# Attention scores of a head pair in one run of half-array products, and a planner with new operation lengths

## The chip, the cores and the metric

The kernel runs on one core of one Trainium2 chip. The metric is the device time of one execution in microseconds; the median of three runs is given. Before the change it is 209.5 us.

## What is computed

The reference has two stages. The first is a recurrent linear attention over 4 batches, 8 heads, 768 positions and a head size of 64. Each head has a decay gamma, and

```
state = gamma * state + k[t] v[t]^T
x[t]  = scale * q[t] state
```

The 8 heads side by side make an x of 768 x 512 for each batch. The second stage is a mixer: with `xt` the transpose of x,

```
h   = relu(xt @ w_tok1) @ w_tok2        # 768 -> 256 -> 768, over positions
u   = x + h^T
out = u + relu(u @ w_ch1) @ w_ch2       # 512 -> 1536 -> 512, over channels
```

## The kernel before, in words

**Tiling of the attention.** The recurrence is done in 6 chunks of 128 positions (NC = 6, HC = 3 is half of them). Two heads make a pair, so each batch has 4 pairs, and one call of `front(b, p)` makes all the instructions of one pair p of one batch b. The keys are scaled by powers of the decay (L419 on ScalarE, L421 on VectorE) and cast; the queries are cast (L427, L429) in batches 2 and 3. Both are then transposed so that the head size lies on the partitions, with one head of the pair on partitions 0 to 63 and the other on 64 to 127: by TensorE in batches 0 and 1 (L454, L456, copied out of PSUM at L463), by DMA transposes from the SyncE queue in batches 2 and 3 (L442). The states of the chunks are products of keys and values (L478), run into each other on VectorE (L487, L490: `U`), and scaled into a block-diagonal tile (L501, L503: `r`).

**The scores.** At L521 keys times queries are formed for each chunk: a product that contracts over 64 partitions only, so that it uses half of the array's rows, and the two heads of a pair use the two halves. The products of three chunks of one head fill 384 of the 512 columns of one PSUM bank. The kernel before makes them in two operations for each pair, one for each half of the sequence (`hf`): six products in turns of the two heads, into two banks. VectorE then multiplies each bank by the causal mask and writes it in half precision (L529, `am`). The Y products (L543 with the states, L546 with the masked scores) follow; X is scaled out of PSUM (L559 on ScalarE, L563 on VectorE) and cast (L576).

**The mixer.** The products over positions stay in `front`: L590 (w_tok1), L600 (relu), L648 (w_tok2), an addition at L655, a cast at L663 and a transpose (L682, L688, or by DMA at L672). In batch 0 they take another form (L615, L618, L625, L770). `back(b)` makes the channel part: `widen` (L738 products, L752 relu on ScalarE), and `narrow` (L778 products, L786 additions); batches 2 and 3 use `narrow_seven` (L854, L863, L896), with seven products in place of eight.

**What sets the order.** Nothing runs in the order in which it is written. Each piece of work is an `Op` with its ways (an engine, a time for which the engine is taken, a time until the result is there), what it depends on, and the tiles and banks that it opens. `arrange()` goes through them like a machine: at each step it takes the operation that can start first, of those the one of the best priority, picks the engine that would be done first where there are two ways, and gives each PSUM tile the bank that comes free first. `replay()` runs the finished order again with a model of the DMA queues and so corrects the landing times that `arrange()` uses. After 16 turns the order with the least planned end is emitted. So a time in a tuple like `dict(ACT=(540, 610), DVE=(410, 465))` decides only the order and the engine. `free` holds the time at which each engine is first available.

**Banks.** In batch 0 the front has banks 0 to 6 ("first"); in the later batches it has banks 0 to 4 ("front") and the back has 5 to 7. An operation that opens a bank waits until all that used it before are done.

**Loads.** Keys, queries, values and weights come through the GpSimd queue (L375, L357), each with a cast to half precision, in one fixed order: batch 0, the weights, then batches 1 to 3. Each request waits for the one eight places ahead of it. The same GpSimd also does the casts of L576 and L663. In the first 30 us zero products (L964) fill gaps that the plan leaves on TensorE.

Of the kernel before, what the change touches and what calls it, by code (L numbers as in the profile page):

```python
# [10 lines left out]
FP = mybir.dt.float32  # L11
F16 = mybir.dt.float16
# [5 lines left out]
def kernel(  # L18
# [11 lines left out]
    nc = tc.nc  # L30
# [23 lines left out]
    SEM = 80  # L54
    XB, XU = 2, 3
    EARLY, BOTH_FIRST, SEVEN = 0, 1, 2
    ops = []
# [25 lines left out]
    def replay(order):  # L83
# [17 lines left out]
        at = {e: 0 for e in lines}  # L101
        free = dict(PE=0, ACT=2500, DVE=0, POOL=850, SP=700)
        dmas = {e: [] for e in ("SP", "POOL", "ACT")}
# [73 lines left out]
    def arrange():  # L177
        free = dict(PE=0, ACT=2500, DVE=0, POOL=850, SP=700)
        gens = [0, 0, 0]
# [87 lines left out]

    def act(n, scaled=False):
        t = 186 + (93 if scaled else 0) + 5 * n // 6
        return t - 60, t + 20  # L270

    def dve(n, per=1.04):
        return int(140 + n * per), int(170 + n * per)

# [92 lines left out]
    rcount = [0]  # L367

    def load(b, p):
        got = []  # L370
        for tag, src in (("kf", k), ("qf", q), ("v16", v)):
            s = Slot(tag)

            def emit(s=s, src=src):
                nc.gpsimd.dma_start(out=tile_of(s, [P, 2, NC, D], F16),  # L375
                                    in_=src[b, 2 * p:2 * p + 2].rearrange("h (c p) d -> p (h c) d", p=P))
            pr = (0, -2) if (b, p) == (0, 0) and tag == "kf" else (0, b, p)
            got.append((s, request(pr, 1040, emit, (96, 13.2), [s])))
        loads[b, p] = got

    def front(b, p):
# [32 lines left out]
        def emit(e, js):  # L414
            t = opened(K, [P, NC, 2, D], F16)
            for j in js:
# [3 lines left out]
                else:  # L420
                    nc.vector.tensor_scalar(t[:, :, j], KF.tile[:, j], gk[:, h:h + 1], None, ALU.mult)  # L421
        kl = parts(emit, dict(ACT=(540, 610), DVE=(410, 465)), [kd, g_op], K, KF, ([0], [1]))

# [6 lines left out]
        if b < XB:  # L430
            ql = [qd]
        else:
            ql = parts(emit, dict(ACT=(780, 860), DVE=(500, 550)), [qd], Q, QF, (slice(0, 2),))

# [3 lines left out]
        def turn(src, dst, dep):  # L438
            if b >= XB:
                def emit():  # L440
                    t = tile_of(dst, [P, S], F16)
                    nc.sync.dma_start_transpose(out=t.rearrange("d (c t) -> d c t", t=P),  # L442
                                                in_=flat(src.tile))
                o = Op((0, b, p, 0), [("SP", 100, 100, emit)], dep, [dst], [src], dma=(48, 24))
                return [o, o]
            T = Slot(FA)

            def emit():
                tp = tile_of(T, [P, 1024], F16)
                for c in range(NC):  # L450
                    o = tp[:, c * P:(c + 1) * P]
                    if src is QF:
                        for j in range(2):
                            nc.tensor.transpose(o[j * D:(j + 1) * D], src.tile[:, j, c], ident16)  # L454
                    else:
                        nc.tensor.transpose(o, src.tile[:, c].rearrange("p h d -> p (h d)"), ident16)  # L456
            t = op(one("PE", (600, 760) if src is QF else (340, 500), emit), dep + [ident_op], [T], [src])

            def emit(e, hs):
                d, o = opened(dst, [P, S], F16), T.tile[:, :S]  # L460
                d = d.rearrange("d (f t) -> d f t", f=2)[:, hs]
                o = o.rearrange("d (f t) -> d f t", f=2)[:, hs]
                (nc.scalar.copy if e == "ACT" else nc.vector.tensor_copy)(d, o)  # L463
            if last:
                return parts(emit, dict(ACT=act(S // 2), DVE=dve(S // 2, 0.54)), [t], dst, T,
                             (slice(0, 1), slice(1, 2)))
            return 2 * parts(emit, dict(ACT=act(S), DVE=dve(S, 0.54)), [t], dst, T, (slice(0, 2),))
# [6 lines left out]
        def emit():  # L474
            st = tile_of(ST, [P, 512], FP)
            for c in range(NC - 1):
                for j in range(2):
                    nc.tensor.matmul(st[j * D:(j + 1) * D, c * D:(c + 1) * D], K.tile[:, c, j],  # L478
                                     V.tile[:, j, c], start=True, stop=True)
        pp = op(one("PE", (320, 470), emit), kl + [vl, two_before], [ST], [K, V])  # L480
        prev = None
        for c in range(NC - 1):
            def emit(c=c):
                o = ST.tile[:, c * D:(c + 1) * D]
                if c == 0:
                    U = tile_of(US, [P, NC - 1, D], FP)
                    nc.vector.tensor_copy(U[:, 0], o)  # L487
                else:
                    U = US.tile
                    nc.vector.scalar_tensor_tensor(U[:, c], U[:, c - 1], gp[:, p:p + 1], o,  # L490
                                                   ALU.mult, ALU.add)
            prev = op(one("DVE", (215, 270), emit), [pp, prev], [US] if c == 0 else [],
                      [ST, US] if c else [ST])

        def emit(e, j):
# [6 lines left out]
            else:  # L502
                nc.vector.tensor_scalar(RS.tile[r, :, r], US.tile[r], g128[2 * p + j], None, ALU.mult)  # L503
        r0 = op(either(lambda e, f=emit: f(e, 0), ACT=(400, 470), DVE=(460, 490)),
                [prev, r16_op], [RS], [US])
        r1 = op(either(lambda e, f=emit: f(e, 1), ACT=(400, 470), DVE=(460, 490)),
                [prev, r0], [], [US, RS])

        AM = [Slot("am") for _ in range(4)]
        am_ops = []  # L510
        for hf in range(2):
            A = [Slot(FA), Slot(FA)]

            def emit(hf=hf, A=A):
                a = [tile_of(A[j], [P, 512], FP)[:, :HC * P].rearrange("p (i t) -> p i t", t=P)
                     for j in range(2)]
                for i in range(HC):
                    t = slice((hf * HC + i) * P, (hf * HC + i + 1) * P)
                    for j in range(2):
                        r = slice(j * D, (j + 1) * D)  # L520
                        nc.tensor.matmul(a[j][:, i], KT.tile[r, t], QT.tile[r, t],  # L521
                                         start=True, stop=True)
            a = op(one("PE", (300, 420), emit), [kt[hf], qt[hf], two_before], A, [KT, QT])
            for j in range(2):
                def emit(hf=hf, j=j, A=A):
                    am = tile_of(AM[2 * hf + j], [P, HC, P], F16)
                    src = A[j].tile[:, :HC * P].rearrange("p (i t) -> p i t", t=P)
                    m = mask1.rearrange("p (o t) -> p o t", o=1).to_broadcast([P, HC, P])
                    nc.vector.tensor_tensor(am, src, m, ALU.mult)  # L529
                am_ops.append(op(one("DVE", (500, 560), emit), [a, mask1_op], [AM[2 * hf + j]], [A[j]]))  # L530
        X16 = Slot("x16")
        x_ops, cast_ops = [], []
        for hf in range(2):
            Y = Slot(FA)

            def emit(hf=hf, Y=Y):
                y = tile_of(Y, [P, 512], FP)
                R = RS.tile
                for i in range(HC):
# [5 lines left out]
                    for j in range(2):  # L545
                        nc.tensor.matmul(o[:, j * D:(j + 1) * D], AM[2 * hf + j].tile[:, i],  # L546
                                         V.tile[:, j, c], start=(c == 0), stop=(c == 0 or j == 1))
            y = op(one("PE", (360, 510), emit), am_ops[2 * hf:2 * hf + 2] + [r0, r1, vl], [Y],
                   [QT, RS, V, AM[2 * hf], AM[2 * hf + 1]])
            y_done[b * NP + p] = y  # L550

            def emit(e, hf=hf, Y=Y):
# [8 lines left out]
                else:  # L561
                    gg = gyw[:, 2 * p:2 * p + 2].rearrange("p (o h) d -> p o (h d)", o=1)
                    nc.vector.tensor_tensor(X.tile[:, half(hf), pc], yv, gg.to_broadcast([P, HC, P]),  # L563
                                            ALU.mult)
            ways = either(emit, ACT=(720, 800)) if first else either(emit, ACT=(720, 800), DVE=(520, 580))
            opens = (b, "X") not in first_of
# [6 lines left out]
            def emit(e, hf=hf):  # L573
                if hf == 0:
                    tile_of(X16, [P, NC, P], F16)
                (nc.vector if e == "DVE" else nc.gpsimd).tensor_copy(  # L576
                    X16.tile[:, half(hf)], X.tile[:, half(hf), pc])
            cast_ops.append(op(either(emit, POOL=(460, 530), DVE=(520, 560)),
                               [ev] + cast_ops, [X16] if hf == 0 else [], [X] if hf == 0 else [X, X16]))
# [60 lines left out]
        for hf in range(2):  # L640
# [12 lines left out]
            def emit(hf=hf, T2=T2):  # L653
                xo = X.tile[:, half(hf), pc]
                nc.vector.tensor_tensor(  # L655
                    xo, xo, T2.tile[:, :HC * P].rearrange("p (i d) -> p i d", d=P), ALU.add)
            ad = op(one("DVE", (500, 560), emit), [t2, cast_ops[hf]], [], [T2, X])
            x_done[b, p, hf] = ad

            def emit(e, hf=hf):  # L660
                if hf == 0:
                    tile_of(U16, [P, NC, P], F16)
                (nc.vector if e == "DVE" else nc.gpsimd).tensor_copy(  # L663
                    U16.tile[:, half(hf)], X.tile[:, half(hf), pc])
            casts.append(op(either(emit, POOL=(460, 530), DVE=(520, 560)),
                            [ad] + casts, [U16] if hf == 0 else [], [X] if hf == 0 else [X, U16]))
# [51 lines left out]
    def back(b):  # L718
# [40 lines left out]
        def narrow(sh):  # L759
            H2, rel = h2_of[sh]  # L760
            for i in range(HC):
# [22 lines left out]
                def emit(sh=sh, i=i, A=A, O=O):  # L784
                    o = tile_of(O, [P, C], FP)
                    nc.vector.tensor_tensor(o, X.tile[:, sh * HC + i], A.tile, ALU.add)  # L786
                ad = op(one("DVE", (640, 700), emit), [last] + [x_done[b, p, sh] for p in range(NP)],
                        [O], [A, X])
# [208 lines left out]
```

## Time and profile before

| what | value |
| --- | --- |
| time, median of 3 runs | 209.5 us (208.44 to 209.69) |
| span of the profiled execution | 208.2 us |
| TensorE clock granted | 0.996 |
| first L738, first product of the channel part | 32.2 us |
| L521, score products | 192, 8 runs of twelve and 16 of six |
| L529, maskings | 64, 549 ns each, 33.3 us |
| last L854 | 203.5 us |

A row of the profile's groups gives line, engine and operation, what is written and read, count, busy time and the mean of one; behind the bar stands the idle time of the engine just before. A row of the chain or of the timeline begins with the start in microseconds from the span's start and the length. Matmuls overlap each other, so the distance between two starts says more on TensorE than a record's length.

### The profile page before, as it was taken

To read this page: it belongs to the slowest core of one execution; us is meant where nothing else is said; L and a number is where in the kernel's file an instruction comes from. 1 tells how busy PE (TensorE), PEld (TensorE's weight loads), DVE (VectorE), ACT (ScalarE), POOL (GpSimd) and SP (SyncE) were. 2 spreads that over 40 slices of the span, in tenths; PEclk is the share of its full clock that TensorE was granted. 3 is DMA by queue.
4 is the path that set the end of the run, shared out by engine and by line. 5 is a ranking of instruction groups with operands and counts; after the bars stand their busy time and mean duration, and the time that the engine had idled before them with its cause. 6 is when DMAs were issued, how large, how long until landed. Compare 5 with 4: busy or idle time off the path is not lost.

```text
span 208.2 us, 5030 instructions
## 1 busy us (share of the span) xinstructions
PE 194.7 (94%) x2032; PEld 131.0 (63%) x2032; DVE 126.4 (61%) x331; ACT 115.2 (55%) x250; POOL 79.1 (38%) x111
## 2 busy tenths in 40 slices
PE   7976999999899798999799999999999999999991
PEld 3553785556667365666577566654666887667880
DVE  7597830048798857968487675812007985037972
ACT  3465896578797654476499350730777102776000
POOL 7995963376999643774033124000000000000000
PEclk9999999999999999999999999999999999999998
DMA  7999999999999999999999614302100033000232
GB/s 47 147 158 161 208 206 207 176 156 152 145 149 149 123 186 146 187 125 217 132 183 116 116 50 91 88 0 101 54 0 0 5 139 146 17 3 2 85 120 101
DMA packets 98199, 23.92 MB, mean 115 GB/s; under 512 B 91008, under 2 KB 95104, under 8 KB 98176
## 3 DMA queue, kind: packets, MB, share of 16 engines
q0 software_dynamic: 78720, 13.37, 95.0%
q1 hardware_dynamic: 16000, 3.93, 17.2%
q10 hardware_dynamic: 3456, 6.29, 8.4%
q8 instruction: 16, 0.26, 0.6%
q14 instruction: 7, 0.06, 0.1%
HBM read 26.74 MB, written 6.29 MB: 159 GB/s over the span
## 4 chain that ended last, share of the span: by engine, by line
PE 51%; DMA 34%; POOL 8%; issue 2%; DVE 2%; DVEq 0%; POOLq 0%
PE bank L738 22%; DMA kf<-in_k_dram 14%; PE bank L854 13%; DMA wc<-in_moe_w_ch_dram 8%; PE bank L778 8%; DMA qT<-q 7%; DMA qf<-in_q_dram 4%; POOL kf L375 3%; POOL qf L375 2%; PE bank L590 2%; PE bank L648 2%; POOL v L375 2%; PE bank L521 1%; POOL x L576 1%; PE bank L546 1%
## 5 line engine op out<-in xcount | busy, mean ns | idle before, releaser
L738 PE MATMUL bank<-uT,wc 128*128 128x384 f16 x384 | 67.8, 326 | 0.1
L752 ACT ACTIVATE h<-bank 128x384 f16<-128x384 f32 x96 | 46.6, 488 | 31.0 <-PE bank L738 18.0
L738 PEld LDWEIGHTS <-wc 128*128 128x128 f16 x384 | 36.1, 98 | 24.3 <-issue 0.7
L778 PE MATMUL bank<-wc,h 128*128 128x512 f16 x144 | 37.1, 380 | 0.0
L529 DVE TENSOR_TENSOR am<-bank,mask 128x384 f16<-128x384 f32 x64 | 33.3, 549 | 6.1 <-PE bank L521 6.0
L559 ACT ACTIVATE X<-bank,gy 128x192 f32<-128x192 f32 x48 | 17.2, 416 | 7.7 <-PE bank L546 7.6
L375 POOL DMA_DIRECT2D kf<-in_k_dram x16 | 16.5, 1031 | 9.2 <-DMA qf<-in_q_dram 4.0
L576 POOL CAST x<-X 128x384 f16<-128x384 f32 x28 | 14.1, 518 | 14.0 <-ACT X L559 11.0
L778 PEld LDWEIGHTS <-h 128*128 128x128 f16 x144 | 12.4, 98 | 10.8
L375 POOL DMA_DIRECT2D qf<-in_q_dram x16 | 16.4, 1024 | 5.6 <-DMA wc<-in_moe_w_ch_dram 3.3
L375 POOL DMA_DIRECT2D v<-in_v_dram x16 | 16.3, 1021 | 5.5 <-DMA kf<-in_k_dram 3.5
L419 ACT ACTIVATE k<-kf,gk 128x384 f16<-128x384 f16 x23 | 13.4, 611 | 8.3 <-DMA kf<-in_k_dram 7.2
L490 DVE SCALAR_TENSOR_TENSOR U<-U,gp,bank 128x64 f32<-128x64 f32 x64 | 17.3, 273 | 0.7
L813 DVE TENSOR_TENSOR kf<-h 128x768 f16<-128x768 f16 x6 | 3.3, 558 | 22.4 <-ACT h L752 22.4
L663 POOL CAST u<-X 128x384 f16<-128x384 f32 x22 | 10.8, 509 | 14.2 <-DVE X L655 14.2
L655 DVE TENSOR_TENSOR X<-X,bank 128x384 f32<-128x384 f32 x24 | 12.2, 549 | 6.0 <-PE bank L648 6.0
L854 PEld LDWEIGHTS <-h 128*128 128x128 f16 x144 | 14.1, 98 | 1.9
L590 PE MATMUL bank<-x,wt 128*128 128x128 f16 x192 | 13.8, 219 | 1.4 <-POOL x L576 0.8
L501 ACT ACTIVATE r<-U 64x320 f16<-64x320 f32 x30 | 14.0, 466 | 2.0 <-DVE U L490 1.3
L421 DVE TENSOR_SCALAR k<-kf,gk 128x384 f16<-128x384 f16 x9 | 4.1, 455 | 17.8 <-DMA kf<-in_k_dram 17.7
L786 DVE TENSOR_TENSOR o<-X,bank 128x512 f32<-128x512 f32 x12 | 8.2, 684 | 10.6 <-PE bank L778 10.6
L590 PEld LDWEIGHTS <-wt 128*128 128x128 f16 x192 | 11.8, 98 | 4.1 <-ACT uT L688 1.1
(84 smaller groups left out, 281.9 us busy)
## 6 DMA issues: line engine op xcount, KB each, us to landing
out_dram<-o ACTq DMA_DIRECT2D x24, 256.0 KB, 2.2
kf<-in_k_dram POOLq DMA_DIRECT2D x16, 192.0 KB, 11.4
qf<-in_q_dram POOLq DMA_DIRECT2D x16, 192.0 KB, 12.4
v<-in_v_dram POOLq DMA_DIRECT2D x16, 192.0 KB, 11.9
wc<-in_moe_w_ch_dram POOLq DMA_DIRECT2D x6, 512.0 KB, 15.4
wt<-in_moe_w_tok_dram POOLq DMA_DIRECT2D x2, 384.0 KB, 9.6
kT<-k SPq DMA_TRANSPOSE x8, 8.2
qT<-q SPq DMA_TRANSPOSE x8, 9.7
```

What stands on the lines that cost most here:

```text
L375: nc.gpsimd.dma_start(out=tile_of(s, [P, 2, NC, D], F16), in_=src[b, 2 * p:2 * p + 2].rearrange("h (c p) d -> p (h c) d", p=P))
L419: nc.scalar.activation(t[:, :, j], KF.tile[:, j], AF.Copy, scale=gk[:, h:h + 1])
L490: nc.vector.scalar_tensor_tensor(U[:, c], U[:, c - 1], gp[:, p:p + 1], o, ALU.mult, ALU.add)
L501: nc.scalar.mul(RS.tile[r, :, r], US.tile[r], g128[2 * p + j])
L529: nc.vector.tensor_tensor(am, src, m, ALU.mult)
L559: nc.scalar.mul(X.tile[:, half(hf), h * D:(h + 1) * D], yv[:, :, j * D:(j + 1) * D], gy[:, h:h + 1])
L576: (nc.vector if e == "DVE" else nc.gpsimd).tensor_copy(X16.tile[:, half(hf)], X.tile[:, half(hf), pc])
L590: nc.tensor.matmul(acc[:, jt * P:(jt + 1) * P], wt1[:, i, jt * P:(jt + 1) * P], X16.tile[:, i], start=(i == 0), stop=(i == NC - 1))
L738: nc.tensor.matmul(acc[:, :SH], w[:, ct, (ft % FW) * P:(ft % FW + 1) * P], UT.tile[:, ct, sh * SH:(sh + 1) * SH], start=(ct == 0), stop=(c ...
L752: nc.scalar.activation(H2.tile[:, ft], A.tile[:, :SH], AF.Relu)
L778: nc.tensor.matmul(A.tile, H2.tile[:, ft, i * P:(i + 1) * P], wc2[ft // FW][:, ft % FW], start=(opens and ft == 0), stop=(ft == NF - 1))
L854: nc.tensor.matmul(bank.tile[:, cols], lhs(f, t), rhs(f), start=(f == 0 and not adds), stop=(f == HF - 1), skip_group_check=adds)
```

## The change

The scores of a pair are made in one operation from batch 1 on (`XS = 1`): twelve half-array products in one run, over four banks, where there were two operations of six products over two banks each. `M4 = 3` is the number of chunks in each of the first two banks; with six chunks the other two have three as well. Batch 0 keeps its two operations. The maskings take their bank and their number of blocks from a list, and the Y products look up in `am_of` where a block lies. The aim is that TensorE changes less often between the whole and the half array.

The rest of the change gives the planner other operation lengths, read from a trace, and another first time for the GpSimd queue (1250 for 850) and for the first two loads. The diff, cut:

```diff
+    XS, M4 = 1, 3
...
-        free = dict(PE=0, ACT=2500, DVE=0, POOL=850, SP=700)
+        free = dict(PE=0, ACT=2500, DVE=0, POOL=1250, SP=700)
...
-    def act(n, scaled=False):
-        t = 186 + (93 if scaled else 0) + 5 * n // 6
-        return t - 60, t + 20
+    def act(n):
+        t = 178 + 81 * n // 100
+        return t - 100, t
...
-        return int(140 + n * per), int(170 + n * per)
+        return int(62 + n * per), int(145 + n * per)
...
+    extra = {(0, 0, "kf"): 34, (0, 0, "qf"): 26}
...
-        kl = parts(emit, dict(ACT=(540, 610), DVE=(410, 465)), [kd, g_op], K, KF, ([0], [1]))
+        kl = parts(emit, dict(ACT=(515, 615), DVE=(240, 320)), [kd, g_op], K, KF, ([0], [1]))
...
-            ql = parts(emit, dict(ACT=(780, 860), DVE=(500, 550)), [qd], Q, QF, (slice(0, 2),))
+            ql = parts(emit, dict(ACT=(740, 835), DVE=(340, 390)), [qd], Q, QF, (slice(0, 2),))
...
-            t = op(one("PE", (600, 760) if src is QF else (340, 500), emit), dep + [ident_op], [T], [src])
+            t = op(one("PE", (480, 640) if src is QF else (340, 500), emit), dep + [ident_op], [T], [src])
...
-        pp = op(one("PE", (320, 470), emit), kl + [vl, two_before], [ST], [K, V])
+        pp = op(one("PE", (375, 525), emit), kl + [vl, two_before], [ST], [K, V])
...
-            prev = op(one("DVE", (215, 270), emit), [pp, prev], [US] if c == 0 else [],
+            prev = op(one("DVE", (190, 273), emit), [pp, prev], [US] if c == 0 else [],
...
-        for hf in range(2):
-            A = [Slot(FA), Slot(FA)]
...
-            a = op(one("PE", (300, 420), emit), [kt[hf], qt[hf], two_before], A, [KT, QT])
...
-                am_ops.append(op(one("DVE", (500, 560), emit), [a, mask1_op], [AM[2 * hf + j]], [A[j]]))
+        if b < XS:
+            runs = [[[(j, hf * HC + i) for i in range(HC)] for j in range(2)] for hf in range(2)]
+        else:
+            runs = [[[(j, c) for c in cs] for cs in (range(M4), range(M4, NC)) for j in range(2)]]
+        for blocks in runs:
+            A = [Slot(FA) for _ in blocks]
...
+                for c in sorted({c for _, c in where}):
                     for j in range(2):
...
+                        a, i = where[j, c]
+                        r, t = slice(j * D, (j + 1) * D), slice(c * P, (c + 1) * P)
+                        nc.tensor.matmul(a.tile[:, i * P:(i + 1) * P], KT.tile[r, t], QT.tile[r, t],
                                          start=True, stop=True)
...
+            a = op(one("PE", (370, 500) if len(blocks) == 2 else (545, 680), emit),
+                   [kt[hf] for hf in hfs] + [qt[hf] for hf in hfs] + [two_before], A, [KT, QT])
...
+                mo = op(one("DVE", (66 + 134 * len(bl), 150 + 134 * len(bl)), emit), [a, mask1_op], [M], [A_])
+                for i, jc in enumerate(bl):
+                    am_of[jc] = M, i, mo
...
-            ways = either(emit, ACT=(720, 800)) if first else either(emit, ACT=(720, 800), DVE=(520, 580))
+            ways = either(emit, ACT=(620, 730)) if first else either(emit, ACT=(620, 730), DVE=(475, 557))
```

The lengths of the state scalings (L501), the Y products, the casts (L576, L663) and the additions (L655, L786) are changed in the same manner.

More of the change, by code (lines that the diff above doesn't have):

```diff
@@ L177, in arrange @@
     def arrange():
-        free = dict(PE=0, ACT=2500, DVE=0, POOL=850, SP=700)
+        free = dict(PE=0, ACT=2500, DVE=0, POOL=1250, SP=700)
         gens = [0, 0, 0]
@@ L377, in load @@
             pr = (0, -2) if (b, p) == (0, 0) and tag == "kf" else (0, b, p)
-            got.append((s, request(pr, 1040, emit, (96, 13.2), [s])))
+            got.append((s, request(pr, 1040, emit, (96 + extra.get((b, p, tag), 0), 13.2), [s])))
         loads[b, p] = got
@@ L503, in emit @@
                 nc.vector.tensor_scalar(RS.tile[r, :, r], US.tile[r], g128[2 * p + j], None, ALU.mult)
-        r0 = op(either(lambda e, f=emit: f(e, 0), ACT=(400, 470), DVE=(460, 490)),
+        r0 = op(either(lambda e, f=emit: f(e, 0), ACT=(365, 467), DVE=(400, 480)),
                 [prev, r16_op], [RS], [US])
-        r1 = op(either(lambda e, f=emit: f(e, 1), ACT=(400, 470), DVE=(460, 490)),
+        r1 = op(either(lambda e, f=emit: f(e, 1), ACT=(365, 467), DVE=(400, 480)),
                 [prev, r0], [], [US, RS])
-        AM = [Slot("am") for _ in range(4)]
@@ L510, in front @@
-        am_ops = []
-        for hf in range(2):
-            A = [Slot(FA), Slot(FA)]
[L514 to L518, printed above, removed]
+        AMW = max(HC, M4)
+        AM, am_ops, am_of = [], [], {}
+        if b < XS:
+            runs = [[[(j, hf * HC + i) for i in range(HC)] for j in range(2)] for hf in range(2)]
+        else:
+            runs = [[[(j, c) for c in cs] for cs in (range(M4), range(M4, NC)) for j in range(2)]]
@@ L519, in emit @@
+        for blocks in runs:
+            A = [Slot(FA) for _ in blocks]
+            def emit(blocks=blocks, A=A):
+                where = {jc: (a, i) for a, bl in zip(A, blocks) for i, jc in enumerate(bl)}
+                for a in A:
+                    tile_of(a, [P, 512], FP)
+                for c in sorted({c for _, c in where}):
                     for j in range(2):
-                        r = slice(j * D, (j + 1) * D)
-                        nc.tensor.matmul(a[j][:, i], KT.tile[r, t], QT.tile[r, t],
+                        a, i = where[j, c]
+                        r, t = slice(j * D, (j + 1) * D), slice(c * P, (c + 1) * P)
+                        nc.tensor.matmul(a.tile[:, i * P:(i + 1) * P], KT.tile[r, t], QT.tile[r, t],
@@ L522, in emit @@
                                          start=True, stop=True)
-            a = op(one("PE", (300, 420), emit), [kt[hf], qt[hf], two_before], A, [KT, QT])
[L524 to L529, printed above, removed]
-                am_ops.append(op(one("DVE", (500, 560), emit), [a, mask1_op], [AM[2 * hf + j]], [A[j]]))
+            hfs = [hf for hf in range(2) if any(c // HC == hf for bl in blocks for _, c in bl)]
@@ new lines, in front, with emit @@
+            a = op(one("PE", (370, 500) if len(blocks) == 2 else (545, 680), emit),
+                   [kt[hf] for hf in hfs] + [qt[hf] for hf in hfs] + [two_before], A, [KT, QT])
+            for A_, bl in zip(A, blocks):
+                M = Slot("am")
+                AM.append(M)
+                def emit(bl=bl, A_=A_, M=M):
+                    m = len(bl)
+                    am = tile_of(M, [P, AMW, P], F16)
+                    src = A_.tile[:, :m * P].rearrange("p (i t) -> p i t", t=P)
+                    k_ = mask1.rearrange("p (o t) -> p o t", o=1).to_broadcast([P, m, P])
+                    nc.vector.tensor_tensor(am[:, :m], src, k_, ALU.mult)
+                mo = op(one("DVE", (66 + 134 * len(bl), 150 + 134 * len(bl)), emit), [a, mask1_op], [M], [A_])
+                for i, jc in enumerate(bl):
+                    am_of[jc] = M, i, mo
@@ L545, in emit @@
                     for j in range(2):
[L546 to L549, printed above, removed]
+                        M, m, _ = am_of[j, c]
+                        nc.tensor.matmul(o[:, j * D:(j + 1) * D], M.tile[:, m], V.tile[:, j, c], start=(c == 0), stop=(c == 0 or j == 1))
+            ms = [am_of[j, hf * HC + i] for j in range(2) for i in range(HC)]
+            mine = [M for M in AM if any(M is m[0] for m in ms)]
+            y = op(one("PE", (345 if hf else 290, 500 if hf else 440), emit),
+                   list({id(m[2]): m[2] for m in ms}.values()) + [r0, r1, vl], [Y], [QT, RS, V] + mine)
             y_done[b * NP + p] = y
@@ L577, in emit @@
                     X16.tile[:, half(hf)], X.tile[:, half(hf), pc])
-            cast_ops.append(op(either(emit, POOL=(460, 530), DVE=(520, 560)),
+            cast_ops.append(op(either(emit, POOL=(450, 510), DVE=(462, 548)),
                                [ev] + cast_ops, [X16] if hf == 0 else [], [X] if hf == 0 else [X, X16]))
@@ L656, in emit @@
                     xo, xo, T2.tile[:, :HC * P].rearrange("p (i d) -> p i d", d=P), ALU.add)
-            ad = op(one("DVE", (500, 560), emit), [t2, cast_ops[hf]], [], [T2, X])
+            ad = op(one("DVE", (465, 548), emit), [t2, cast_ops[hf]], [], [T2, X])
             x_done[b, p, hf] = ad
@@ L664, in emit @@
                     U16.tile[:, half(hf)], X.tile[:, half(hf), pc])
-            casts.append(op(either(emit, POOL=(460, 530), DVE=(520, 560)),
+            casts.append(op(either(emit, POOL=(450, 510), DVE=(462, 548)),
                             [ad] + casts, [U16] if hf == 0 else [], [X] if hf == 0 else [X, U16]))
@@ L786, in emit @@
                     nc.vector.tensor_tensor(o, X.tile[:, sh * HC + i], A.tile, ALU.add)
-                ad = op(one("DVE", (640, 700), emit), [last] + [x_done[b, p, sh] for p in range(NP)],
+                ad = op(one("DVE", (605, 687), emit), [last] + [x_done[b, p, sh] for p in range(NP)],
                         [O], [A, X])
```

## The prediction

> **What bounds the kernel now.** I read the page first: busy shares, slices, queues.
>
> ```profile
> PE 194.7 (94%) x2032; PEld 131.0 (63%) x2032; DVE 126.4 (61%) x331; ACT 115.2 (55%) x250; POOL 79.1 (38%) x111
> ...
> PE   7976999999899798999799999999999999999991
> ...
> DMA  7999999999999999999999614302100033000232
> ...
> q0 software_dynamic: 78720, 13.37, 95.0%
> ```
>
> TensorE is nearly always busy, and the DMA rings are full up to slice 22, some 114 us. A busy TensorE is not proof of work, since each record overlaps the next, so I took the distance from one matmul's start to the next as its price. The TensorE timeline gives 0.163 us for L738, 0.216 for L778, 0.056 for the 128-column products of L590, L648 and L682. Counts times these pitches, from the first L738 at 32.2 us to the last L854 at 203.6, come to 164.9 us of work; the stretch lasts 171.4, so 6.5 us in it are waits. Then 4.6 us of additions and the output's store follow. TensorE sets the end, and what can be won is work taken off it, or these waits.
>
> The chain that ended last says what the waits are (start, length, what):
>
> ```profile
> 61.02 18.48 DMA kf<-in_k_dram
> 79.52 0.32 DVE k L421
> 79.84 0.48 DVE X L563
> 80.36 0.32 PE bank L521 x5
> ...
> 91.40 10.62 DMA qT<-q
> 102.02 0.14 issue
> 102.16 0.51 PE bank L521 x12
> ...
> 114.62 4.66 DMA qT<-q
> ```
>
> Two kinds: a load that arrives late and holds VectorE, whose next instruction would have freed a bank for a score run; and a transposed query that reaches the score run itself late. Before 102 us the waits cost 5.8 us: the largest lie at 55 (1.0), 71 to 73 (1.4) and 80.4 (1.2). The one at 102.16 costs 1.3, later ones 0.5. The rows of TensorE's waits agree:
>
> ```profile
> PE bank L521 <- DMA qT<-q: 2.0, 3, 1.2
> ...
> PE bank L521 <- DVE X L563: 1.0, 1, 1.0
> ...
> PE bank L590 <- POOL x L576: 0.8, 1, 0.8
> ```
>
> The score runs themselves, in the timeline (start, us, engine, line):
>
> ```profile
> 83.59 0.59 PE L778 MATMUL bank<-wc,h 128*128 128x512 f16 x2
> 84.12 0.34 PE L521 MATMUL bank<-qT,kT 64*128 64x128 f16 x6
> 84.39 1.04 PE L778 MATMUL bank<-wc,h 128*128 128x512 f16 x4
> ...
> 107.97 0.51 PE L521 MATMUL bank<-qT,kT 64*128 64x128 f16 x12
> 108.41 0.84 PE L590 MATMUL bank<-x,wt 128*128 128x128 f16 x12
> ```
>
> Two L778 take 0.43 us, but the score run starts 0.53 after the first: 0.10 us go into the change from the whole to the half array. Six products then hold TensorE for 0.27 us, twelve for 0.44. So the second six cost 0.17 and about 0.10 is paid on leaving.
>
> **What the skill says.** "TensorEngine Tiling (Array Packing)", Tiling Modes: changing the tiling mode, not merely the tile, drains TensorE. The trace agrees: about 0.10 us at each end of a half-array run. Same page, Restrictions and Gotchas: different row tiles write different PSUM banks and may not use one bank at once. That is why the two heads of a pair have banks of their own, and why one run for the pair takes four. "PSUM — Partial Sum Buffer", Engine vs sequencer instructions: the queues of ScalarE, VectorE and GpSimd are strict FIFO. The chain agrees: at 79.5 us VectorE's L563 stood behind a key scaling that waited for its load. "DMA: Bandwidth & Descriptors", Issuing engines are not separate DMA queues: transfers from all issuers share the same 16 engines and interleave. The trace agrees: a transpose issued at 91.40 landed 10.62 us later, beside the loads.
>
> **The change part by part.**
>
> *The merged run.* With HC = M4 = 3, a bank holds three blocks as before and each of the 64 maskings (L529, 549 ns) keeps its shape: nothing is added or taken on VectorE. Before, eight of the sixteen pairs already have a run of twelve (the four of batch 0, and four later ones which the planner put together); eight have two runs of six. A merge saves 2 x (0.10 + 0.27) - (0.10 + 0.44) = 0.20 us; eight make 1.6. Some half-array runs stand beside others, where entering costs nothing, so I counted in the order of the built programs: half-array groups fall from 48 to 40, entries from the whole array from 39 to 34. That is 8 x 0.10 + 5 x 0.10 = 1.3 us, all of it TensorE work on the path. With the pitches, the work from the first L738 on falls from 164.9 to 163.7 us. I take 1.2.
>
> *The added wait.* A run now opens four of the five front banks at once, and waits for both halves of kT and qT; these come in one transfer or copy in the later batches, so the second costs nothing. On TensorE everything queued behind, the back products too, waits with it; the maskings, then the Y products, wait for the run. In the changed order the TensorE work between a bank's last writer and the score run that reopens it is at least 1.26 us, mostly 1.5 to 5; before, three cases lie at 1.1 to 1.3. The low bound is no wait. The high bound is the shortest succession, pairs 2 and 3 of batch 1, 2.8 us of work apart: four maskings at a pitch of 0.47 take 1.9, and one load in VectorE's queue ahead of them can add 1 us. I take 0, for the reason two parts below.
>
> *The new lengths.* They change no instruction, only the order, and the choice between engines. Query casts on VectorE go from 2 to 6 (0.384 us there, 0.828 on ScalarE), key scalings from 9 to 11 (about 0.32 against 0.61), X scalings from 8 to 5 (0.555). Together with the copies VectorE gets about 1 us more and ScalarE half a us less; both are under 62% busy, so the sums are hidden. Two zero products more (0.16 each) lie in the first 23 us where TensorE waits for loads: nothing.
>
> *The order against the loads.* The rings are full whatever the plan, so I hold the landings and move the work. For a score run, let A be the TensorE work between the first L738 and it. TensorE can't be there before the query lands, so landing minus A is a floor under first L738 plus all waits so far. Batch 3, pair 0: A is 63.9 us before, which gives 102.16 - 63.9 = 38.3, and the end follows: 38.3 + 164.9 + 0.4 of later waits = 203.6, as measured. In the changed order A is 64.7, since the fronts of batches 1 and 2 stand 2 to 4 us later among the back products. The floor is 102.16 - 64.7 = 37.5. All waits before this point, a bank wait included, only eat into a lead which TensorE would have to wait off here; that is why I took 0 above, and why I count nothing for the 2.6 us at 71 to 80 either, though most of them should go. The end is then 37.5 + 163.7 + 0.4 = 201.6: 2.0 us won, 1.2 by less work and 0.8 by the place of the run.
>
> *The query itself.* For that pair the cast ran on ScalarE at 90.54, behind two key scalings and a scaling of X, and its transpose left at 91.40. It is now on VectorE and less than half as long. The transpose can't leave ahead of the pair's kT, which went at 89.75: the gain is between 0 and 1.65 us. I take 1.0. Sum: 3.0 us, 209.5 - 3.0 = 206.5.
>
> **The rivals.**
>
> *A, the waits stay.* The loads come later by what the order gains, because the transposes of the other pairs interleave differently; only the 1.2 us of work go: 208.3. For it: full rings up to 114 us. Against it: the floor's arithmetic, which needs no faster transfer for the 0.8.
>
> *B, slower: the wait moves to VectorE's queue.* Six query casts and eleven key scalings there now wait directly for loads, with maskings and additions behind them. In the changed order the cast of pair 2 of batch 2 stands ahead of the additions of batch 1, the cast of pair 1 ahead of the maskings of batch 1. The case at 79.5 held 2.7 us of idle VectorE and cost TensorE 1.2. If four such come, at 1.3 each, and push back the scalings that feed the transposes so that the floor rises with them, 5.2 us are lost against the 3.0: 211.7. Against it: the plan now expects the first loads 0.4 us later than it did, near to what the trace shows, so it leaves more room.
>
> *C, more won.* If the batch 3 queries of pairs 0 to 2 come early enough, the last one binds: it landed at 119.28, A there is 83.9 in the changed order, floor 119.4 - 83.9 = 35.5, end 35.5 + 163.7 = 199.2, 4.4 us won: 205.1.
>
> **How the numbers follow.** Forecast 206.5 with 0.50; A 208.3 with 0.27; B 211.7 with 0.13; C 205.1 with 0.10. The likeliest is 206.5. The range leaves out most of B and little of C: 204.5 to 210.0. Faster by over 1% means under 207.4: nearly all of the forecast, C and a little of A, less the part of the forecast in which the query gains nothing, 0.55. Same 0.33, slower 0.12.
>
> **What would show it.** In the profile after: score runs of twelve alone, about 0.44 us from start to next start; the maskings still x64 at 549 ns; TensorE's waits between 50 and 81 us well under 4 us; a wait for qT at the first pair of batch 3 (a little before 102 us), and the first L738 about where it was. The prediction is wrong if that wait for qT is absent and another one, on VectorE or a bank, has come instead; if TensorE waits for a bank at score runs; or if qT of batch 3 lands later than 102 us.

## The result, and the profile after

The changed kernel takes 206.4 us (median of 4 runs) against 209.2 us before (a fourth run joined the three): a ratio of 0.987, 95% interval 0.983 to 0.991. Run once more beside the later experiments it gave 0.987 again (0.981 to 0.993). The forecast was 206.5, which was 3.0 us under the 209.5 known then; measured are 2.8. Times and ratios here and below leave out slow executions, those more than 1.5% above the fastest of the same kernel.

The page of the changed kernel: first the busy shares, then the maskings (line, engine, operation, count, busy time, mean ns, idle before), which are L544 now; the score products are L530, the channel products L757, L797 and L873. In the text, L738 and L854 stand for the first and the last kind of channel product in every kernel.

```profile
PE 193.8 (95%) x2034; PEld 132.0 (64%) x2034; DVE 128.2 (63%) x335; ACT 116.0 (57%) x252; POOL 78.4 (38%) x108
...
DMA  6999999999999999999999733202100133000222
...
q0 software_dynamic: 78720, 13.37, 96.6%
...
L544 DVE TENSOR_TENSOR am<-bank,mask 128x384 f16<-128x384 f32 x64 | 32.7, 548 | 3.8 <-PE bank L530 3.7
```

The rings are as full as before, to slice 22; VectorE has 1.8 us more and ScalarE 0.8 more (foreseen were about 1 more and half a us less; both stay hidden), and the maskings have kept their shape. The timeline of TensorE (start, us) shows the merged run among channel products:

```profile
116.64 0.51 PE L530 MATMUL bank<-qT,kT 64*128 64x128 f16 x12
117.08 1.25 PE L797 MATMUL bank<-wc,h 128*128 128x512 f16 x5
```

It is 0.44 us from its start to the next start, the price that a run of twelve had before. All runs have twelve now. What TensorE waited for at the score runs, from the waits (total, times, longest):

```profile
PE bank L530 <- DVE U L493: 0.9, 1, 0.9
...
PE bank L530 <- DMA qT<-q: 0.7, 2, 0.4
```

And the chain that ended last, in the stretch from 60 to 108 us:

```profile
60.75 19.80 DMA kf<-in_k_dram
80.55 0.02 issue
80.57 0.32 DVE k L424
80.89 0.20 DVE U L493
...
81.78 0.47 PE bank L530 x6
...
97.23 9.66 DMA qT<-q
106.90 0.04 issue
106.94 0.51 PE bank L530 x12
```

The first wait is one for a bank: in the middle of a merged run the third bank was still held by state products, whose reader on VectorE stood behind a key scaling that waited for a load. The second is the transposed query of batch 3, pair 1: it landed at 106.90 and the score run began 0.04 us later. Pair 0 had waited for its own query at 100.6 (0.32 us).

From starts and pitches, as in the prediction, TensorE's time from the first L738 (now L757) to the last L854 (now L873) comes apart into work and waits:

| kernel | first L738 | last L854 | work between | waits between |
| --- | --- | --- | --- | --- |
| before | 32.2 | 203.5 | 165.1 | 6.2 |
| changed | 33.3 | 200.1 | 163.8 | 2.9 |
| changed, run again | 33.1 | 201.2 | 163.8 | 4.3 |

Work fell by 1.3 us; the waits fell by 1.9 to 3.3 us; the stretch starts about 1 us later. Each row is one execution: the one of the kernel before took 210.0 us, 0.8 over its median, so its waits may be at the high end.

### The profile page after: what moved, and what is told of

It reads as the page before. It is cut to its first block, busy times and chain, and to the rows that moved or that the text cites. A ratio compares the mean times of both kernels' runs of the same rounds, so it can differ in the third digit from the quotient of the medians.

```text
span 204.8 us, 5035 instructions
## 1 busy us (share of the span) xinstructions
PE 193.8 (95%) x2034; PEld 132.0 (64%) x2034; DVE 128.2 (63%) x335; ACT 116.0 (57%) x252; POOL 78.4 (38%) x108
## 4 chain that ended last, share of the span: by engine, by line
PE 63%; DMA 19%; DVE 10%; POOL 4%; issue 1%; ACT 1%; DVEq 0%; POOLq 0%
PE bank L757 25%; PE bank L873 13%; PE bank L797 11%; DMA kf<-in_k_dram 10%; DMA qT<-q 5%; DMA v<-in_v_dram 4%; PE bank L609 3%; DVE am L544 3%; DVE U L493 2%; PE bank L667 2%; PE bank L564 2%; POOL kf L378 2%; PE bank L530 1%; POOL qf L378 1%; DVE k L424 1%; PE bank L634 1%
## 5 line engine op out<-in xcount | busy, mean ns | idle before, releaser
L757 PE MATMUL bank<-uT,wc 128*128 128x384 f16 x384 | 67.8, 326 | 0.0
L757 PEld LDWEIGHTS <-wc 128*128 128x128 f16 x384 | 36.1, 98 | 23.4 <-issue 0.3
L797 PE MATMUL bank<-wc,h 128*128 128x512 f16 x144 | 36.5, 380 | 0.0
L544 DVE TENSOR_TENSOR am<-bank,mask 128x384 f16<-128x384 f32 x64 | 32.7, 548 | 3.8 <-PE bank L530 3.7
L578 ACT ACTIVATE X<-bank,gy 128x192 f32<-128x192 f32 x54 | 19.4, 417 | 10.7 <-PE bank L564 10.3
L797 PEld LDWEIGHTS <-h 128*128 128x128 f16 x144 | 12.5, 98 | 10.8
L595 POOL CAST x<-X 128x384 f16<-128x384 f32 x26 | 13.3, 516 | 15.8 <-ACT X L578 12.3
L682 POOL CAST u<-X 128x384 f16<-128x384 f32 x21 | 10.5, 517 | 16.1 <-DVE X L674 16.1
L422 ACT ACTIVATE k<-kf,gk 128x384 f16<-128x384 f16 x21 | 12.4, 610 | 6.5 <-DMA kf<-in_k_dram 6.3
L873 PEld LDWEIGHTS <-h 128*128 128x128 f16 x144 | 14.1, 98 | 1.8
L564 PEld LDWEIGHTS <-am 128*128 128x128 f16 x192 | 12.4, 100 | 3.3 <-issue 1.5
L564 PE MATMUL bank<-v,am 128*128 128x64 f16 x192 | 14.4, 197 | 0.1
L424 DVE TENSOR_SCALAR k<-kf,gk 128x384 f16<-128x384 f16 x11 | 5.9, 534 | 13.2 <-DMA kf<-in_k_dram 13.2
```

The costliest lines, as they stand in the source:

```text
L422: nc.scalar.activation(t[:, :, j], KF.tile[:, j], AF.Copy, scale=gk[:, h:h + 1])
L544: nc.vector.tensor_tensor(am[:, :m], src, k_, ALU.mult)
L564: nc.tensor.matmul(o[:, j * D:(j + 1) * D], M.tile[:, m], V.tile[:, j, c], start=(c == 0), stop=(c == 0 or j == 1))
L578: nc.scalar.mul(X.tile[:, half(hf), h * D:(h + 1) * D], yv[:, :, j * D:(j + 1) * D], gy[:, h:h + 1])
L595: (nc.vector if e == "DVE" else nc.gpsimd).tensor_copy(X16.tile[:, half(hf)], X.tile[:, half(hf), pc])
L757: nc.tensor.matmul(acc[:, :SH], w[:, ct, (ft % FW) * P:(ft % FW + 1) * P], UT.tile[:, ct, sh * SH:(sh + 1) * SH], start=(ct == 0), stop=(c ...
```

## The experiments

**The two parts of the change alone.** My theory had the floor under the late queries as the cause: where the runs of batch 3 stand among TensorE's work. Its rival was the fit of the whole plan. Both halves of the change were run.

The merge alone: the code of the changed kernel with every operation length of before, and

```diff
-            a = op(one("PE", (370, 500) if len(blocks) == 2 else (545, 680), emit),
+            a = op(one("PE", (300, 420) if len(blocks) == 2 else (475, 600), emit),
```

> The merged score run with the planner's old operation lengths (the merged run itself planned at 475 and 600, its maskings as before). The order is another one: the TensorE work between the first L738 and the score run of batch 3 is 69.0, 74.3, 81.2 and 85.3 us for its four pairs (64.8, 70.6, 80.3 and 84.0 in the changed kernel). Theory of the floor (landing of the transposed query minus that work sets the end): with landings as before, 102.0, 107.5, 114.4, 119.3, the floors are 33.0, 33.2, 33.2 and 34.0 us, no longer above first L738 plus other waits; then 163.7 us of work give a last L854 at 198 to 199.5 us, a span near 203.5 and a time near 205.0, not slower than the changed kernel. Rival (the new lengths make the plan fit the chip, the merge by itself only adds bank waits): slower than the changed kernel, 208 or more, with waits of over 4 us after the first L738.

Measured: 0.9936 of before (0.9911 to 0.9961), 208.5 us. The floor theory fell here: its 205 was missed by 3.5 us, and the rival's number came out. Work is 163.7 us, as with the whole change, but the waits are 5.3 us. They lie earlier than I looked. The chain of this kernel:

```profile
61.35 20.36 DMA qf<-in_q_dram
81.71 0.02 issue
81.73 0.11 ACT q L430
81.84 0.63 issue
82.47 0.39 ACT h L619
82.86 0.04 issue
82.90 0.83 PE bank L667 x12
```

A query of batch 2 is cast on ScalarE; the cast waits for its load until 81.71, and a relu for another pair stands behind it, for which TensorE waits about 1 us. The largest of its waits has another way:

```profile
PE bank L701 <- POOL u L682: 1.6, 1, 1.6
```

This one ends at 75.3 us. The cast on GpSimd (L682) stood behind the request for a load, before which that queue had been idle for 3.7 us. There is not one floor but many: a load, or the request for one, that an engine's queue waits for sets one, through whatever stands behind it.

The lengths alone:

```diff
-    XS, M4 = 1, 3
+    XS, M4 = 4, 3
```

> The new lengths with two runs of six in every batch (XS = 4). Work ahead of the score runs of batch 3: 64.3, 70.5, 77.4, 81.5 us; 164.8 us of work from the first L738. Theory of the floor: pair 0 lands near 100.5 to 102.0 and pair 1 near 106.9, floor 36.3 to 37.7, last L854 at 201.2 to 202.6, time 207.5 to 208.5: the changed kernel plus the 1.1 us of array changes. Rival (bank waits of the four-bank run cost what the merge saves): as fast as the changed kernel, 206.4. Rival (the new lengths bring nothing by themselves): as before, 209.2.

Measured: 0.9985 (0.9955 to 1.0015), 209.1 us against 209.6: no difference from before. Work is 165.2 us, waits are 3.6 in the profiled execution (208.0 us, one of its fastest), the largest 1.4 at 91.4 us, where the last pair of batch 2 waited for its query. It is slower than the floor theory said; that the lengths bring nothing by themselves is what the timing supports.

**Work moved about in the changed order.** If TensorE only waits less when it comes later to the late loads, work put ahead of them is free and the same work put behind them is not. One L738 product is repeated six times (0.98 us), first in batch 0:

```diff
                     for ct in cts:
-                        nc.tensor.matmul(...)
+                        for more in range(6 if (b, sh, ft, ct) == (0, 0, 4, 0) else 0, -1, -1):
+                            nc.tensor.matmul(...)
```

> The changed kernel, same order, with one L738 product of batch 0 repeated six times (0.98 us of TensorE work) ahead of the score runs that wait for the queries of batch 3. Theory of the floor: TensorE only waits less at those two runs (0.32 and 0.51 us of wait in the changed kernel), so the time rises by 0.1 to 0.3 us, to 206.6. Rival (TensorE's sum sets the end, the loads do not): plus 1.0 us, 207.4.

Then in batch 2, `(2, 0, 1, 0)`, behind all score runs:

> The changed kernel, same order, with one L738 product of batch 2 repeated six times (0.98 us of TensorE work) after all score runs, at about 141 us. Both theories: plus 1.0 us, 207.4; it is the measure against which the early repetition is read.

And twelve products fewer in batch 0:

```diff
+                        if b == 0 and sh == 0 and 4 <= ft < 10 and ct in (1, 2):
+                            continue
```

> The changed kernel, same order, with twelve L738 products of batch 0 left out (for six of its column blocks the two middle ones of four products, so the channel part of batch 0 is summed over half of the channels there): 1.95 us of TensorE work less, all of it between 34 and 43 us, ahead of every score run that waits for a load. Theory of the floor: TensorE only reaches the late loads sooner and waits there; the time falls by 0 to 0.4 us. Rival (TensorE's sum sets the end): by 1.9 us.

For comparison, the changed kernel as it is:

> The changed kernel once more, beside these: 206.4 us, the measure for the early repetition, the late one, the cut and the two plans.

Measured, with the places from each trace (the query is that of batch 3, pair 1):

| kernel | ratio to before | query landed | its run began | last L854 | from the run to the last L854 |
| --- | --- | --- | --- | --- | --- |
| changed | 0.9869 (0.9829 to 0.9910) | 106.90 | 106.94 | 200.07 | 93.13 |
| changed, again | 0.9865 (0.9805 to 0.9925) | 107.92 | 107.97 | 201.21 | 93.24 |
| 0.98 us more, early | 0.9841 (0.9790 to 0.9892) | 106.36 | 106.40 | 199.53 | 93.13 |
| 0.98 us more, late | 0.9899 (0.9838 to 0.9961) | 108.00 | 108.04 | 202.15 | 94.11 |
| 1.95 us less, early | 0.9953 (0.9931 to 0.9975) | 108.88 | 108.92 | 202.05 | 93.13 |

In all five executions the run begins 0.04 or 0.05 us after its query has landed, and the end follows at a distance that is fixed to 0.1 us, longer by 0.98 us where the work was put behind. No cost of the early repetition is seen, and taking work away early won nothing. The intervals of the first four ratios overlap, so what settles this is the traces, one of each. In three of the five TensorE is seen to wait at this run: 0.51 us in the changed kernel, 0.51 with more work early, 0.87 with less. The execution with more work early helped itself: its first L738 came at 32.36 us, for 33.31 in the changed kernel, so TensorE stood at the same place after the repetition. What it shows is that there was still a wait to absorb the work. The chain with more work early, and then with less:

```profile
96.99 9.36 DMA qT<-q
106.36 0.04 issue
106.40 0.51 PE bank L530 x12
```

```profile
99.36 9.51 DMA qT<-q
108.88 0.04 issue
108.92 0.51 PE bank L530 x12
```

In the two others TensorE waits 0.07 us at this run or not at all, so that it begins so soon after the landing there is partly chance; a late load is felt one step sooner. The chain of the changed kernel run again:

```profile
77.06 21.43 DMA qf<-in_q_dram
98.49 0.02 issue
98.52 0.83 ACT q L430
```

The load of that pair's query landed at 98.49 (94.25 in the first profile); ScalarE's cast waited for it, the relus behind the cast held the channel part's banks (0.8 us of wait at 100.4), and the transpose left late as well.

So the landing is no constant: 106.4 to 108.9 in one and the same order. With less early work it came latest, and the kernel was slower by about 1% than with more. Its first transpose left at 58.9 us, for 59.9 in the changed kernel, so the transposes meet the loads in another order. That this is what made the loads late was not tried; it stays open.

**The pace of the loads in the plan.** A load of a pair's keys, queries or values is planned at 96 x 13.2 = 1.27 us. In the changed kernel's profile, from the key load of batch 1, pair 0 (42.15 us) to the value load of batch 2, pair 1 (65.05), 17 loads land in 22.9 us, 1.35 each. So the plan expects the data of batches 2 and 3 too soon. Two paces were changed, that of a load alone and that of loads and transposes beside each other (`BOTH`), three numbers in all:

```diff
-    BESIDE, BOTH = 0.25, dict(SP=57, POOL=37)
+    BESIDE, BOTH = 0.25, dict(SP=62, POOL=40)
...
-            got.append((s, request(pr, 1040, emit, (96 + extra.get((b, p, tag), 0), 13.2), [s])))
+            got.append((s, request(pr, 1040, emit, (96 + extra.get((b, p, tag), 0), 14.1), [s])))
```

> The changed kernel with two numbers of the planner's model of the loads made like the trace: 14.1 for 13.2 (a load of 192 KB each 1.35 us for 1.27; the trace shows 1.36), and the pace beside a transpose SP 62 for 57, POOL 40 for 37. Only the order changes. Theory (the plan places work of batches 2 and 3 ahead of loads that land 2 to 4 us later than it believes; the waits come from that): work ahead of the score runs of batch 3 is 68.0, 78.2, 84.1 and 89.6 us, against 64.8, 70.6, 80.3 and 84.0; floors with the changed kernel's landings are 32.5, 28.8, 29.6 and 26.2 us, all under the first L738; waits after the first L738 fall from 2.9 to about 1 us, and the time to 204.5. Rival (these orders differ by luck, the pace in the plan has no part in it): within 1 us of the changed kernel, either way.

Measured: 0.9752 (0.9706 to 0.9798), 204.3 us. The execution that was profiled took 209.3 us, so its waits are not read here. Then with `dict(SP=66, POOL=43)`:

> As the last, with SP 66 and POOL 43 beside a transpose. Work ahead of the score runs of batch 3: 69.4, 79.2, 86.1 and 93.3 us. Theory of the plan's pace: as fast as the last or a little faster, 204 to 204.5, unless the last fronts now stand so late that the channel part of batch 2 waits for them. Rival (luck): within 1 us of the changed kernel.

Measured: 203.1 us, 0.9678 (0.9644 to 0.9713), faster than both kernels. The waits of this kernel:

```profile
PE bank L459 <- DVE k L424: 1.3, 3, 0.7
PE bank L983 <- DVE zero L304: 1.1, 1, 1.1
PE bank L530 <- ACT r L504: 0.2, 1, 0.2
```

None is a wait for a bank in a channel stage or for a query of batches 2 and 3, and all three rows belong to the start: after the first L738 starts and pitches leave 0.2 us of waits in all. The busy times by stage (stretch, its length, TensorE's busy time and matmuls, weight loads, VectorE, ScalarE, GpSimd, clock, rings, GB/s), first of the changed kernel, then of this one:

```profile
33.30:80.00 46.70, 46.40 (x562) 30.24 (x561) 31.32 (x83) 33.59 (x72) 31.86 (x38) 1.00 2.46 157
80.00:120.00 40.00, 38.45 (x495) 26.05 (x493) 31.54 (x80) 25.75 (x57) 17.21 (x28) 1.00 1.65 159
```

```profile
30.00:80.00 50.00, 50.00 (x606) 32.82 (x603) 29.65 (x81) 38.19 (x81) 33.84 (x42) 1.00 2.40 161
80.00:120.00 40.00, 40.00 (x476) 25.96 (x473) 28.53 (x72) 25.42 (x58) 16.28 (x26) 1.00 1.59 163
```

The rings move bytes at nearly the same rate; TensorE has no idle time left in these stretches. The load's own pace without the pace beside a transpose:

> The changed kernel with 14.1 for 13.2 alone, the pace beside a transpose as it was. Work ahead of the score runs of batch 3: 65.4, 75.2, 81.4, 87.1 us; the loads beside transposes still land 1 to 2 us later than planned. Theory: pair 0 still binds (landing near 101 to 102, floor 36), 206; the pace beside transposes is what e6 and e7 added. Rival: the load pace does it alone, 204 or less.

Measured: 0.9890 (0.9846 to 0.9934), 206.9 us: no better than the changed kernel's 0.987. The row of its waits:

```profile
PE bank L530 <- DMA qT<-q: 3.7, 2, 2.5
```

These are pair 1 of batch 2 at 79.5 (2.6 us, not foreseen) and pair 0 of batch 3 at 102.3 (1.3, foreseen). So the pace beside a transpose is needed. Whether it would do alone, with 13.2 left as it was, was not run.

**What the pace leaves to the two parts.** The same three numbers without the merge, without the new lengths, and without either:

> The planner's pace of the last run (14.1, SP 66, POOL 43) and the new lengths, but two runs of six in every batch. 164.9 us of TensorE work from the first L738, against 163.75 with the merge. Theory (with no waits left, TensorE's work sets the end): 1.2 us over the 203.1 of the run with the merge, 204.3. Rival (the four-bank run hampers the front and gives its saving back): 203 or less.

> The pace and the merge, with the planner's old operation lengths; 163.85 us of work. Theory (the waits come from the pace of the loads in the plan, the operation lengths matter little): 203.2. Rival (both the lengths and the pace are needed for a plan that the chip follows): 205 or more, with waits after the first L738 of 2 us or more.

> The kernel before with the pace alone: two runs of six, old lengths; 164.5 us of work in its order. Theory: the pace removes most of the 6.2 us of waits, 204 to 204.5, more than the whole change brought. Rival: the old lengths keep over 3 us of waits, 207.

| plan | ratio to before | work | waits |
| --- | --- | --- | --- |
| pace alone, on the kernel before | 0.9815 (0.9794 to 0.9836) | 164.7 | 1.2 |
| pace and lengths | 0.9808 (0.9785 to 0.9832) | 165.1 | 0.8 |
| pace and merge | 0.9771 (0.9729 to 0.9814) | 164.0 | 0.2 |
| pace, lengths and merge | 0.9678 (0.9644 to 0.9713) | 163.8 | 0.2 |

The pace alone brings 1.9%, the whole change 1.3%, with intervals that just meet. In all four plans the waits are 1.2 us or less, where the orders with the old pace beside a transpose have 2.4 or more in their profiles; that these orders differ by mere luck is hard to hold against this. With the pace the lengths by themselves bring nothing again. The merge is worth 1.3% beside the new lengths, clear of the intervals. That is 2.7 us: 1.3 of work and 0.6 of waits in the profiles, the rest is not accounted for. Without the lengths the intervals meet, but the work is less by 0.7 us there, because the planner had already joined half-runs of some pairs (44 half-array groups, not 48).

One thing goes against "the lengths bring nothing": beside the merge they do. They take 0.9936 to 0.9869 without the pace and 0.9771 to 0.9678 with it, both times just clear of the intervals. In the two paced profiles work and waits differ by only 0.2 us and the last L854 by 0.5 us, so where the 0.9% comes from is not shown.

## Why the prediction was right

**The work taken off TensorE** was put at 1.2 us from 8 x 0.10 + 5 x 0.10 = 1.3. Right: 165.1 to 163.8. The merge alone agrees, with 163.7 us of work and 1.3 us less time, though its order and waits are others too.

**The added bank wait** was taken as 0 with 1 us as high bound, "one load in VectorE's queue". Half right: it came, 1.0 us at 81.8, and in that very way, though as a state bank held by VectorE and not in the succession of the two pairs of batch 1. A wait for a bank at a score run was one of the signs by which the prediction was to be known as wrong; the sign came. The wait did not reach the end, since TensorE waited later for a query anyway. That such waits are absorbed agrees with the early repetition: with a us of work added there TensorE still waited for that query.

**The floor** was computed for pair 0 of batch 3: 37.5 less 1.0 for the earlier query, 36.5. Measured: the query landed at 100.47, 1.55 us earlier, and the run began at 100.61, a floor of 35.9. The step that was missed is pair 1: the work ahead of it is 70.5 us, so its start at 106.94 makes a floor of 36.4, and that one binds. 36.4 + 163.7 = 200.1, which is where the last L854 stands. The sum is right to 0.5 us because pair 1 took the place that I gave to pair 0: that its floor came out 0.1 us from the one forecast for pair 0 is luck. No later wait of 0.4 came. (One slip in the prediction's account of before: its 5.8 us of waits must include the 1.3 at 102.16, or they do not fit 6.5 in all.)

**"I hold the landings and move the work"** is the weak step. It happened to hold to 1 or 2 us, but the landing that binds moved between 106.4 and 108.9 in five executions of the same order, and with less work early it came later. Nor does the floor of batch 3 foretell other orders: for the merge alone it gave 205.0 where 208.5 was measured, since waits before 83 us bound instead.

**The new lengths** were said to change only the order, with 0.8 us from the place of the runs and 1.0 from the query's cast. The gain in time beyond the work is there with both parts together, and neither part alone has it: it belongs to the orders that both together make. Rival A (only the work is won) is what the merge alone did. Rival B was seen in small, as the bank wait; rival C did not come.

**The first L738** was expected where it was; it came 1.1 us later in the first profile and 0.9 in the second, behind a late load of batch 0 each time, as told below. It was absorbed too.

What the prediction did not see is why there were waits to win: the plan believes in transfers faster than those of the trace. The code has 96 x 13.2 = 1.27 us for a load where landings are 1.35 us apart, and I did not make that comparison. By itself it would not have been enough: the load's pace alone gave 0.9890, and the gain came with the pace beside a transpose.

## What to carry to other kernels

Where an order is planned ahead, compare the plan's own numbers with the trace before anything else, and those of the transfers first: three numbers for the pace of transfers brought 1.9% alone, where some twenty lengths of operations brought nothing measurable alone and 0.7 to 0.9% beside the merge. For a late transfer, count the work that stands ahead of its first user and behind it: work ahead is absorbed up to the size of the wait, work behind counts in full, and each in-order queue that waits for a load makes such a point of its own. A saving in TensorE's work can count in full once no such point binds: with the pace and the new lengths the merged run's 1.3 us of work came with 2.7 us of time.

## What the runs showed of the hardware that I had not expected

In the changed kernel's profile the value load of batch 0, pair 2 landed at 18.36 us, 2.9 us behind the load before it, while most are 1.3 to 1.5 apart; before it had landed at 16.86. TensorE waited 1.7 us for it, until 18.40. From 17.9 us on, still in the wait, the clock granted to it was half, for 3.4 us (stretch, length, TensorE, weight loads, VectorE, ScalarE, GpSimd, clock, rings, GB/s):

```profile
15.00:18.00 3.00, 1.49 (x21) 0.77 (x19) 2.62 (x7) 2.65 (x7) 1.87 (x3) 0.99 2.45 156
18.00:19.50 1.50, 1.10 (x22) 0.90 (x22) 0.38 (x2) 0.00 (x0) 0.61 (x1) 0.50 2.38 164
19.50:21.50 2.00, 2.00 (x29) 1.79 (x27) 1.48 (x5) 1.70 (x5) 1.60 (x4) 0.54 1.67 191
21.50:23.00 1.50, 1.49 (x32) 0.98 (x32) 1.19 (x4) 1.05 (x3) 1.50 (x3) 1.00 1.20 212
```

In these 3.4 us L564 and L459 products start 0.07 and 0.11 us apart, for 0.03 and 0.06 elsewhere. A short wait can cost a second time in this way, but its length alone does not tell. In the profile with less work early a wait of 1.16 us up to 18.25 went with 3.4 us of half clock, from 18.2 us on; in the kernel before, 1.22 us up to 19.7 did not, and with the load's own pace alone 2.5 us up to 79.5 did not. What decides it is not shown. Nor did the late first L738 need it: in the changed kernel's second profile the clock stayed full there, a key load of batch 0 landed 2.9 us behind the load before it, and the first L738 came at 33.1 us all the same. And a DMA transpose of one tile, 128 x 768 in half precision, took 7.3 to 10.7 us from issue to landing beside the loads of the changed kernel, and 2.7 to 4.1 us at their end and after them.
